# The attention rows of a chunk are transposed by DMA inside SBUF, and its query products stand in one run

## The chip, the cores and the metric

The kernel runs on one core of one Trainium2 chip. The metric is the device time of one execution in microseconds (us). Every time below is from that, or from one profiled execution of the same program.

## What is computed

The reference has three parts, one after another.

```python
# 1. linear attention: batch 8, heads 8, sequence 576, head width 64
kv = einsum('bhsd,bhse->bhde', k, v)
out = einsum('bhsd,bhde->bhse', q, kv)
out = out / sqrt(mean(out * out, axis=-1) + 1e-6) * g_norm
x = out.transpose(0, 2, 1, 3).reshape(4608, 512)
# 2. a dense layer with a maximum over three products, 512 -> 768 -> 512
h = maximum(maximum(x @ w1, x @ w2), x @ w3)
x = h @ w_out
# 3. a mixture of 8 experts, top 2 of noisy logits, 512 -> 1024 -> 512 each
out[token] = sum over its two experts of weight * (maximum(x @ W1[e], 0) @ W2[e])
```

## The kernel before

Tokens are worked on in nine chunks (0 to 8) of 512. Every matrix is split into a high part and a rest, and a product is taken as three products (high-high, high-rest, rest-high).

For a chunk, the dense layer has two stages. In the first, the loop over `g` makes 18 steps of 12 matmuls on TensorE (line 311, `g1_mm`). Three steps give one 128-wide slice of `h`: ScalarE copies the first step's bank into `hm`, VectorE takes the maximum with the next two, and `hsplit` splits the result (lines 315 and 319). Step 17 completes the last slice. In the second stage, `window(c)`, TensorE makes the output product for four blocks `i` of 128 tokens (line 357, `g2`, 36 matmuls each), and the results are copied out of their banks as 16-bit planes (line 364). Each `g2` block takes two of the four banks `AC`, in a ring (`abank`), so block 3 needs the banks of block 1.

The attention of chunk c+1 is worked in between during chunk c. `kv_pair` at step 10 makes the key-value matrix, `ao` multiplies it with the queries (line 214, 64 matmuls for half a chunk), `norm` scales the rows (`norm_a`: square on ScalarE and sum on VectorE; `norm_b1`, `norm_b2`: small operations; `norm_c`: scaling on VectorE), and `xtrans` brings the normed rows into the layout that the next first stage reads: four TensorE transposes into a bank (line 273), then a rounded copy on ScalarE (line 277) and a subtraction on VectorE (line 282). In chunks 1 to 7 half of the rows are made at step 14 and transposed in the window behind block 1; the other half's query products are in the window, and its rows are transposed in the middle of block 3. The order on each engine is the order of the program text; only chunk 0 has a planner. In chunk 1 the first stage works on 256 tokens, since the other 256 were done during chunk 0.

DMAs of the SP queue load queries (into the tile `RB`), keys and values (`KV0` and the tiles `G`) and the gate noise one chunk ahead. Pool's queue scatters the finished rows of a chunk into `Xg` in DRAM (line 427, at steps 10 and 14 of the next chunk) and, in chunk 2's program text, fills the output with zeros (`zero_out`, lines 540 and 543). In the third part `load_rows` reads rows back with a transposing DMA (line 755) as planes of 16-bit halves, and `utrans` copies these together again (line 790), rounds and subtracts (lines 793 and 794).

Of the kernel before, what the change touches and what calls it, by code (L numbers as in the profile page):

```python
# [7 lines left out]
F = mybir.dt.float32  # L8
# [4 lines left out]
U16 = mybir.dt.uint16  # L13
U64 = mybir.dt.uint64
AF = mybir.ActivationFunctionType
OP = mybir.AluOpType
# [4 lines left out]
NCH, CT = 9, 512  # L21
# [64 lines left out]
def body(tc, A, dbg=None):  # L86
    nc = tc.nc
    PE, ACT, DVE, POOL, SP = nc.tensor, nc.scalar, nc.vector, nc.gpsimd, nc.sync
# [8 lines left out]
    def st(name, shape, dt=F):  # L97
        return sb.tile(shape, dt, name=name)
# [5 lines left out]
    STG = [st(f"G{i}", [128, 2048]) for i in range(3)]  # L104
    B0, B1 = (st(f"B{i}", [128, 4096], FR) for i in range(2))
    B2 = st("B2", [128, 2048], FR)
    RA, RB = st("RA", [128, 4 * XW]), st("RB", [128, 4 * XW])
    KB = [sb1.tile([128, 256], F, name=f"kvt{i}") for i in range(2)]
    KV0 = sb1.tile([128, 2048], F, name="kv0")
# [4 lines left out]
    gn = st("gn", [128, 1])  # L114
# [9 lines left out]
    def hbank():  # L124
        cnt["h"] += 1
        return HB[(cnt["h"] - 1) % 4]

    def abank():
        cnt["a"] += 1
        return AC[(cnt["a"] - 1) % 4]  # L130
# [37 lines left out]
    def qv(c):  # L168
        return qbuf[c][:, 0:2048].rearrange("p (a t) -> p a t", a=4)
# [33 lines left out]
    def ao(c, j, banks):  # L203
        for h in range(2):
            ao_bank[c, 2 * j + h] = banks[h]
        for i in range(2):
            t0 = (2 * j + i) * 128
            for p in range(4):
                o = slice(i * 256 + p * 64, i * 256 + (p + 1) * 64)
                for x in range(2):  # L210
                    t = t0 + x * 64
                    kb = KB[(c * CT + t) // S % 2]
                    for h in range(2):
                        PE.matmul(banks[h][HALF[x], o], qv(c)[HALF[h], p, t:t + 64],  # L214
                                  kb[HALF[h], p * 64:(p + 1) * 64], start=True, stop=True)

    xn_of = {}
# [4 lines left out]
    def norm_a(c, i, x=None):  # L222
        if x is None:
            x = XNS[xn_n[0] % 4]
            xn_n[0] += 1
        norm_sq(c, i, x)
        norm_red(c, i)

    def norm_sq(c, i, x):
        xn_of[c, i] = x  # L230
        ACT.activation(x, ao_bank[c, i], AF.Square)
# [5 lines left out]
    def norm_b1(c, i0, i1):  # L237
        s = [ST[:, r, i0:i1, :] for r in range(2)]
        DVE.tensor_scalar(s[0], s[0], 1.0 / 64, 1e-6, op0=OP.mult, op1=OP.add)
        ACT.activation(s[1], s[0], AF.Ln)  # L240
        ACT.activation(s[1], s[1], AF.Exp, scale=-0.5)

    def norm_b2(c, i0, i1):
        s = [ST[:, r, i0:i1, :] for r in range(4)]
        DVE.tensor_tensor(s[2], s[1], s[1], op=OP.mult)
        DVE.scalar_tensor_tensor(s[2], s[2], -0.5, s[0], op0=OP.mult, op1=OP.mult)
        DVE.scalar_tensor_tensor(s[3], s[2], 1.5, s[1], op0=OP.add, op1=OP.mult)

    def norm_c(c, i):
        x = xn_of[c, i]  # L250
        DVE.tensor_tensor(x.rearrange("p (h e) -> p h e", h=8),
                          ao_bank[c, i].rearrange("p (h e) -> p h e", h=8),
                          ST[:, 3, i, :].unsqueeze(2).to_broadcast([128, 8, 64]), op=OP.mult)

    def norm(c, i, x=None):
        norm_a(c, i, x)
        norm_b1(c, i, i + 1)
        norm_b2(c, i, i + 1)
        norm_c(c, i)

    def xview(a, b):
        return [v.rearrange("p (k t) -> p k t", k=4) for v in (a, b)]

    xT = xview(B0[:, 0:2048], B0[:, 2048:4096])
# [20 lines left out]
    def xtrans(c, i):  # L285
        t = xtrans_pe(c, i)
        xtrans_hi(i, t)
        xtrans_lo(i, t)


    def split(src, w):
        ACT.activation(w[:, 0:1024], src, AF.Copy)  # L292
# [55 lines left out]
    def g2(c, i, f0, f1):  # L348
        if f0 == 0:
            x2b[i] = abank(), abank()  # L350
        s = slice(i * 128, (i + 1) * 128)
        for f in range(f0, f1):
            h = hTf(f)
            w = wo(f // 2)[:, :, f % 2]
            for n, (a, b) in enumerate(((0, 0), (0, 1), (1, 0))):
                for z, (lo, hi) in enumerate(((0, 256), (256, 528))):
                    PE.matmul(x2b[i][z][:, 0:hi - lo], h[:, a, s], w[:, b, lo:hi],  # L357
                              start=f == 0 and n == 0, stop=f == 5 and n == 2)
        if f1 == 6:
            DVE.tensor_copy(lgs[:, i, :], x2b[i][1][:, 256:272])  # L360
            for z in range(2):
                b = x2b[i][z].bitcast(U16).rearrange("p (n t) -> p n t", t=2)
                for q in range(2):
                    (ACT.copy if q else DVE.tensor_copy)(  # L364
                        planes[:, i, q * 512 + z * 256:q * 512 + z * 256 + 256], b[:, 0:256, q])
# [417 lines left out]
    def utrans(u, i, tight=False):  # L783
        s = slice(i * 128, (i + 1) * 128)
        pl = rplanes(u)
        g = MG[mgn[0] % 2]
        mgn[0] += 1
        h = g.bitcast(U16).rearrange("p (k t z) -> p k t z", k=4, z=2)
        for q in range(2):
            (ACT.copy if q and not tight else DVE.tensor_copy)(h[:, :, :, q], pl[:, 4 * q:4 * q + 4, s])  # L790
        t = g.rearrange("p (k t) -> p k t", k=4)
        x = xTu[u % 2]
        ACT.activation(x[0][:, :, s], t, AF.Copy)  # L793
        DVE.tensor_tensor(x[1][:, :, s], t, x[0][:, :, s].bitcast(F), op=OP.subtract)  # L794
        if i == units[u] - 1:
            m = units[u]
            DVE.tensor_copy(wid[u % 3][:, 0:m], gt[u % 3][:, 0:m, 0])
            DVE.tensor_copy(idt[u % 3][:, 0:m], gt[u % 3][:, 0:m, 1])
# [25 lines left out]
    def misc1(c, g):  # L824
        if c == 1 and g == 0:
            POOL.memset(STG[2][64:128, 0:1024], 0.0)
            fills()
        if c == 1 and (g == 0 or 8 < g < 14):
            f = max(g - 8, 0)
            hsplit(f, early(f), 0, 256)  # L830
        if c == 2 and g == 2:
            zero_out()
        if g == 0:
            SP.dma_start(noise[c % 2], A["noise"][c])
        if g == 0 and 0 < c < NCH - 1:
            load_q(c + 1)
            if c + 1 < NB:
                for i in range(3):
                    load_kv(c + 1, i)
        if c > 0:  # L840
            if g == 1:
                route_a(c - 1)
            if g == (7 if c == 1 else 10):
                route_b(c - 1)
                scatter(c - 1, 0)
            if g == (12 if c == 1 else 14):
                scatter(c - 1, 1)
        if 0 < c < NB - 1 and g == 10:
            bank = abank()
            for p in range(4):  # L850
                kv_pair(c + 1, p, bank)
            kv_out(c + 1, bank)
        if 0 < c < NCH - 1 and g == 14:
            ao(c + 1, 0, [abank(), abank()])
            for i in range(2):
                norm(c + 1, i)
        if c == NCH - 1:
            if g == 11:
                spec_pick()
                load_regs(0, spi[0:1, 0:1], spi[0:1, 1:2])  # L860
                regE[1] = regE[0]
                regS[1] = SP.value_load(spi[0:1, 2:3], min_val=0, max_val=DUMMY)
                for p in range(3):
                    load_pair(p)
            if g == 12:
                load_rows(0)
            if g in (13, 14, 15, 16, 17):
                splits(1)

    def window(c):  # L870
        nx = c + 1 < NCH

        def fill(i):
            if nx:
                if i == 0:
                    ao(c + 1, 1, [hbank(), hbank()])
                norm(c + 1, i + 2)

        def trans(i):
            xtrans(c + 1, i) if nx else utrans(0, i)  # L880

        if c == 0:
            for i in (2, 3):
                g2(0, i, 0, 3)
                trans(i)
                g2(0, i, 3, 6)
            xn_n[0] = 0
            return
        for i in range(4):
            g2(c, i, 0, 3)  # L890
            if nx and i == 3:
                trans(2)
                trans(3)
            g2(c, i, 3, 6)
            if nx and i == 1:
                trans(0)
                trans(1)
                fill(0)
                fill(1)
            if not nx:  # L900
                if i < 2:
                    trans(2 * i)
                    trans(2 * i + 1)
                if i == 1:
                    load_rows(1)
                splits(1)
# [15 lines left out]
    c = NCH - 1  # L922
# [337 lines left out]
```

## Time and profile before

| | us |
|---|---|
| median of 3 runs | 1556.95 (1556.66 to 1558.84) |
| the profiled execution | 1555.75 |
| its span in the trace | 1554.0 |
| TensorE busy | 1515.0 |
| VectorE busy | 792.4 |
| ScalarE busy | 646.0 |
| Pool busy | 221.4 |

The span is the time from the first to the last instruction in the trace. The busy time of an engine is the sum of its instructions; it is an average over stages. In the rows below, PE is TensorE, PEld its weight load, DVE VectorE, ACT ScalarE, POOL GpSimd and SP the queue that issues most DMAs.

### The profile page before, as it was taken

To read this page: it belongs to the slowest core of one execution; us is meant where nothing else is said; L and a number is where in the kernel's file an instruction comes from. 1 tells how busy PE (TensorE), PEld (TensorE's weight loads), DVE (VectorE), ACT (ScalarE), POOL (GpSimd) and SP (SyncE) were. 2 spreads that over 40 slices of the span, in tenths; PEclk is the share of its full clock that TensorE was granted. 3 is DMA by queue.
4 is the path that set the end of the run, shared out by engine and by line. 5 is a ranking of instruction groups with operands and counts; after the bars stand their busy time and mean duration, and the time that the engine had idled before them with its cause. 6 is when DMAs were issued, how large, how long until landed. Compare 5 with 4: busy or idle time off the path is not lost.

```text
span 1554.0 us, 23767 instructions
## 1 busy us (share of the span) xinstructions
PE 1515.0 (97%) x9564; PEld 1306.2 (84%) x9564; DVE 792.4 (51%) x1573; ACT 646.0 (42%) x1036; POOL 221.4 (14%) x326
## 2 busy tenths in 40 slices
PE   5999999999999999999999999999999999999997
PEld 4789989898989898888888787778888888888886
DVE  5985534343534343457454456465463554535443
ACT  3544322231313131343454445455464554645544
POOL 0000211111020202024211102101021010211102
PEclk8999999999999999999999999999999999999999
DMA  7322643031212101063676477766695666858554
GB/s 295 134 82 90 254 197 116 29 117 42 103 56 89 56 29 56 1 191 123 205 196 143 109 223 184 169 209 171 162 222 132 196 161 165 202 150 217 148 157 77
DMA packets 132292, 219.82 MB, mean 141 GB/s; under 512 B 96464, under 2 KB 96720, under 8 KB 114640
## 3 DMA queue, kind: packets, MB, share of 16 engines
q1 hardware_dynamic: 112320, 166.50, 34.0%
q0 software_dynamic: 19856, 51.73, 14.7%
q8 instruction: 77, 1.26, 0.3%
q14 instruction: 39, 0.32, 0.1%
HBM read 146.30 MB, written 51.72 MB: 127 GB/s over the span
## 4 chain that ended last, share of the span: by engine, by line
PE 92%; DVE 3%; ACT 2%; DMA 1%; issue 1%; POOL 1%; SPq 0%; POOLq 0%; ACTq 0%
PE bank L311 28%; PE bank L1068 24%; PE bank L1130 24%; PE bank L357 10%; PE bank L192 1%; PE bank L214 1%; PE bank L273 1%; DVE mg L790 1%; ACT B L793 1%; DMA pad<-kvr 1%; PE bank L1082 1%; DMA G<-kv 0%; POOL Xg L427 0%; DVE xlo L794 0%; PE bank L501 0%
## 5 line engine op out<-in xcount | busy, mean ns | idle before, releaser
L311 PE MATMUL bank<-B,W 128*128 128x512 f32 (+1 forms) x2160 | 455.5, 372 | 6.6 <-ACT W L482 4.2
L311 PEld LDWEIGHTS bank<-B,W 128*128 128x128 f32 x2160 | 377.6, 190 | 75.8 <-ACT W L482 4.9
L1130 PE MATMUL bank<-W,B 128*128 128x512 f32 x1728 | 423.3, 392 | 2.0 <-ACT xn L1135 1.9
L1130 PEld LDWEIGHTS bank<-W,B 128*128 128x128 f32 x1728 | 321.2, 189 | 67.0 <-ACT xn L1135 2.3
L1068 PE MATMUL bank<-B,W 128*128 128x512 f32 (+1 forms) x1728 | 355.0, 343 | 6.9 <-ACT B L793 6.9
L1068 PEld LDWEIGHTS bank<-B,W 128*128 128x128 f32 x1728 | 280.9, 190 | 51.1 <-ACT B L793 8.7
L293 DVE TENSOR_TENSOR W<-G,W 128x1024 fp32r<-128x1024 f32 x200 | 242.1, 1223 | 120.2 <-ACT W L292 119.6
L292 ACT ACTIVATE W<-G 128x1024 fp32r<-128x1024 f32 x200 | 207.6, 1055 | 53.3 <-PE bank L1130 39.8
L1073 DVE SCALAR_TENSOR_TENSOR B<-bank,B 128x512 fp32r<-128x512 f32 (+1 forms) x176 | 103.8, 592 | 207.1 <-ACT B L1072 206.6
L1072 ACT ACTIVATE B<-bank 128x512 fp32r<-128x512 f32 (+1 forms) x176 | 90.4, 516 | 266.7 <-PE bank L1068 265.5
L357 PE MATMUL bank<-W,B 128*128 128x256 f32 (+1 forms) x1296 | 164.0, 286 | 0.0
L357 PEld LDWEIGHTS bank<-W,B 128*128 128x128 f32 x1296 | 160.2, 188 | 1.1
L427 POOL DMA_INDIRECT Xg<-RA,si x72 | 72.1, 1001 | 522.1 <-issue 378.1
L329 DVE TENSOR_TENSOR hm<-hm,bank 128x512 f32<-128x512 f32 (+1 forms) x106 | 69.5, 656 | 132.3 <-PE bank L311 125.6
L315 ACT ACTIVATE B<-hm 128x512 fp32r<-128x512 f32 (+1 forms) x53 | 32.2, 607 | 184.7 <-DVE hm L329 184.7
L1068 PE MATMUL bank<-xlo,W 128*128 128x512 f32 x384 | 103.2, 391 | 0.0
L1104 POOL DMA_INDIRECT out<-xn,idt x37 | 61.3, 1655 | 275.3 <-ACT xn L1135 268.3
L1068 PEld LDWEIGHTS bank<-xlo,W 128*128 128x128 f32 x384 | 72.3, 188 | 15.1
L793 ACT ACTIVATE B<-mg 128x512 fp32r<-128x512 f32 x76 | 48.0, 632 | 84.4 <-DVE mg L790 84.3
L1104 POOL DMA_INDIRECT out<-x2T,idt x19 | 30.4, 1602 | 266.0 <-ACT x2T L1135 263.6
L364 ACT COPY RA<-bank 128x256 uint16<-128x256 uint16 x72 | 25.7, 372 | 88.0 <-DVE RA L364 72.7
L794 DVE TENSOR_TENSOR xlo<-mg,B 128x512 fp32r<-128x512 f32 x49 | 34.0, 694 | 36.7 <-ACT B L793 36.7
(184 smaller groups left out, 1010.4 us busy)
## 6 DMA issues: line engine op xcount, KB each, us to landing
G<-mw SPq DMA_DIRECT2D x100, 1024.0 KB, 5.1
G<-w1s SPq DMA_DIRECT2D x12, 1024.0 KB, 4.9
out<-pad POOLq DMA_DIRECT2D x1, 9472.0 KB
kv<-kv SPq DMA_DIRECT2D x8, 1024.0 KB, 7.2
G<-kv SPq DMA_DIRECT2D x8, 1024.0 KB, 9.7
RB<-qT SPq DMA_DIRECT2D x8, 1024.0 KB, 5.1
G<-kvr SPq DMA_DIRECT2D x7, 256.0 KB, 9.8
Xg<-RA,si POOLq DMA_INDIRECT x72, 2.7
```

Source lines behind the costliest of these rows:

```text
L292: ACT.activation(w[:, 0:1024], src, AF.Copy)
L293: DVE.tensor_tensor(w[:, 1024:2048], src, w[:, 0:1024].bitcast(F), op=OP.subtract)
L311: PE.matmul(bank[:, 0:t1 - t0], w_in(g)[:, a, k, s], x[b][:, k, t0:t1], start=n == 0 and k == 0, stop=n == 2 and k == 3)
L329: DVE.tensor_tensor(hm, hm, bank, op=OP.max)
L357: PE.matmul(x2b[i][z][:, 0:hi - lo], h[:, a, s], w[:, b, lo:hi], start=f == 0 and n == 0, stop=f == 5 and n == 2)
L427: i = POOL.indirect_dma_start(out=Xg, out_offset=bass.IndirectOffsetOnAxis(ap=idx, axis=0), in_=src, in_offset=None)
L793: ACT.activation(x[0][:, :, s], t, AF.Copy)
L1068: PE.matmul(bank[:, 0:n], w[:, a, k, s], x[b][:, k, 0:n], start=z == 0, stop=z == 11)
L1072: ACT.activation(h[:, 0, 0:n], bank[:, 0:n], AF.Relu)
L1073: DVE.scalar_tensor_tensor(h[:, 1, 0:n], bank[:, 0:n], 0.0, h[:, 0, 0:n].bitcast(F), op0=OP.max, op1=OP.subtract)
L1104: d = POOL.indirect_dma_start(out=A["out"], out_offset=bass.IndirectOffsetOnAxis(ap=idt[u % 3][:, i:i + 1], axis=0), in_=y, in_offset=None ...
L1130: PE.matmul(obank[i], h[:, a, s], w[:, b, ff % 2, :], start=ff == 0 and n == 0, stop=ff == 7 and n == 2)
```

## The change

From chunk 2 on, the TensorE transposes are gone. `planes_out` copies the low and the high 16-bit halves of a block of normed rows apart, into `KV0` (one half on VectorE, one on ScalarE). `planes_turn` issues a transposing DMA from `KV0` to `RB` on SP's queue, 128 partitions by 2048 halves, one for two blocks. `planes_in` puts the halves together again in a `G` tile and makes the rounded part and the rest from there. `attend` spreads the attention of a chunk over steps 12 to 15: all query products and the first two squares at 12, the other two and the small operations at 13, scaling and halves and a DMA at 14 and at 15. In the window `planes_in` comes behind output blocks 0 and 1. Chunks 0 and 1 keep the TensorE transposes.

```diff
+    def xplanes(c):
+        return [t.bitcast(U16)[:, 0:4096] for t in (KV0, RB)]
+
+    def planes_out(c, b):
+        d = xplanes(c)[0].rearrange("p (b z k i e) -> p b z i k e", b=4, z=2, k=2, i=2)
+        x = xn_of[c, b].bitcast(U16).rearrange("p (i k e z) -> p z i k e", i=2, k=2, z=2)
+        for z in range(2):
+            (ACT.copy if z else DVE.tensor_copy)(d[:, b, z], x[:, z])
+
+    def planes_turn(c, j):
+        src, dst = xplanes(c)
+        SP.dma_start_transpose(out=dst[:, j * 2048:(j + 1) * 2048].rearrange("p (q t) -> p q t", q=16),
+                               in_=src[:, j * 2048:(j + 1) * 2048])
+
+    def planes_in(c, b):
+        p = xplanes(c)[1].rearrange("p (b z n) -> p b z n", b=4, z=2)
+        m = STG[c % 2][:, b * 512:(b + 1) * 512]
+        h = m.bitcast(U16).rearrange("p (n z) -> p n z", z=2)
+        for z in range(2):
+            (ACT.copy if z else DVE.tensor_copy)(h[:, :, z], p[:, b, z])
+        j, k = divmod(b, 2)
+        m = m.rearrange("p (k t) -> p k t", k=2)
+        hi, lo = (x[:, 2 * k:2 * k + 2, j * 256:j * 256 + 256] for x in xT)
+        ACT.activation(hi, m, AF.Copy, scale=gn[:, 0:1])
+        DVE.scalar_tensor_tensor(lo, m, gn[:, 0:1], hi.bitcast(F), op0=OP.mult, op1=OP.subtract)
+
+    def attend(c, n):
+        if n == 0:
+            for j in range(2):
+                ao(c, j, [abank(), abank()])
+        if n < 2:
+            for b in (2 * n, 2 * n + 1):
+                norm_a(c, b)
+        if n == 1:
+            norm_b1(c, 0, 4)
+            norm_b2(c, 0, 4)
+        if n in (2, 3):
+            j = n - 2
+            for b in (2 * j, 2 * j + 1):
+                norm_c(c, b)
+                planes_out(c, b)
+            planes_turn(c, j)
...
-        if 0 < c < NCH - 1 and g == 14:
-            ao(c + 1, 0, [abank(), abank()])
-            for i in range(2):
-                norm(c + 1, i)
+        if 0 < c < NCH - 1 and g >= 12:
+            attend(c + 1, g - 12)
...
         for i in range(4):
-            g2(c, i, 0, 3)
-            if nx and i == 3:
-                trans(2)
-                trans(3)
-            g2(c, i, 3, 6)
-            if nx and i == 1:
-                trans(0)
-                trans(1)
-                fill(0)
-                fill(1)
+            g2(c, i, 0, 6)
+            if i < 2:
+                for b in (2 * i, 2 * i + 1):
+                    if nx:
+                        planes_in(c + 1, b)
+                    else:
+                        utrans(0, b)
```

## Rows read from the trace of the kernel before

**Rows 1.** The page, part 1: busy us, share of the span, instructions.

```profile
PE 1515.0 (97%) x9564; PEld 1306.2 (84%) x9564; DVE 792.4 (51%) x1573; ACT 646.0 (42%) x1036; POOL 221.4 (14%) x326
```

**Rows 2.** The chain that ended last, chunk 5: start us, us, what.

```profile
416.87 27.22 PE bank L311 x120
...
469.94 8.79 PE bank L357 x72
478.72 0.87 PE bank L273 x8
479.59 1.09 PE bank L214 x64
...
487.48 0.97 PE bank L273 x8
...
490.67 9.54 PE bank L311 x42
```

**Rows 3.** Groups by line: out<-in, shapes, count, busy us, mean ns, idle before.

```profile
L790 ACT COPY mg<-RB 128x512 uint16<-128x512 uint16 x41 | 31.6, 771 | 0.0
L790 DVE COPY mg<-RB 128x512 uint16<-128x512 uint16 x65 | 28.3, 455 | 0.0
...
L251 DVE TENSOR_TENSOR xn<-bank,stat 128x512 f32<-128x512 f32 x25 | 17.1, 691 | 2.3
...
L273 PE MATMUL bank<-cst,xn 128*128 128x128 f32 x100 | 15.3, 276 | 0.7 <-DVE xn L251 0.7
```

**Rows 4.** Busy time of each engine over chunk 5 (PE, PEld, DVE, ACT, POOL).

```profile
416.87:490.67 73.80, 73.80 (x587) 64.36 (x587) 31.39 (x94) 19.43 (x41) 8.42 (x16) 1.00 0.20 73
```

**Rows 5.** DMA queues from 699 to 704: GB/s by slice, packets and MB, landing us.

```profile
GB/s 0 0 0 0 0 0 0 0 0 0 0 0 0 0 16 111 156 102 162 201 256 233 268 291 291 285 293 291 291 289 291 293 285 291 293 291 289 289 295 285
...
q1 hardware_dynamic: 3142, 0.80, 72.5%
...
RB<-Xg SPq DMA_TRANSPOSE x1, 6.0
```

**Rows 6.** DMA issues from 671 to 683: us from issue to landing.

```profile
RB<-Xg SPq DMA_TRANSPOSE x1, 17.1
```

**Rows 7.** The chain that ended last, chunk 1's window and chunk 2's start.

```profile
174.81 8.79 PE bank L357 x72
...
195.53 4.55 PE bank L311 x20
```

**Rows 8.** Pool's timeline around 172: start us, us, instruction.

```profile
171.73 2.02 POOL L540 DMA_DIRECT2D out<-pad  x1
```

**Rows 9.** The page, part 6: sizes of Pool's two fills.

```profile
out<-pad POOLq DMA_DIRECT2D x1, 9472.0 KB
...
Xg<-pad POOLq DMA_DIRECT2D x1, 1040.0 KB
```

**Rows 10.** DMA queues from 174.6 to 182: packets, MB, share of 16 engines.

```profile
q0 software_dynamic: 735, 3.01, 101.6%
```

**Rows 11.** DMA issues from 185 to 191: KB, us to landing.

```profile
RB<-qT SPq DMA_DIRECT2D x1, 1024.0 KB, 11.1
```

**Rows 12.** The page, part 6: all such loads, median us to landing.

```profile
RB<-qT SPq DMA_DIRECT2D x8, 1024.0 KB, 5.1
```

**Rows 13.** DMA queues from 205 to 206: packets, MB, share of 16 engines.

```profile
q0 software_dynamic: 95, 0.39, 94.4%
q1 hardware_dynamic: 94, 0.02, 9.4%
```

**Rows 14.** DMA queues from 685 to 687.

```profile
q0 software_dynamic: 120, 0.41, 74.0%
q1 hardware_dynamic: 280, 0.07, 21.6%
```

**Rows 15.** TensorE's timeline around 31: start us, us, form, count, idle before.

```profile
30.95 5.55 PE L311 MATMUL bank<-B,W 128*128 128x512 f32 x16 [4.20 <-ACT W L482]
```

**Rows 16.** Busy time from 30 to 35; the seventh figure is the granted clock.

```profile
30.00:35.00 5.00, 4.05 (x11) 3.19 (x12) 4.92 (x7) 2.07 (x2) 0.00 (x0) 0.69 0.72 272
```

More of the change, by code (lines that the diff above doesn't have):

```diff
@@ L871, in window @@
         nx = c + 1 < NCH
[L873 to L880, printed above, removed]
         if c == 0:
@@ L884, in window @@
                 g2(0, i, 0, 3)
-                trans(i)
+                xtrans(1, i)
                 g2(0, i, 3, 6)
@@ L889, in window @@
         for i in range(4):
-            g2(c, i, 0, 3)
-            if nx and i == 3:
-                trans(2)
-                trans(3)
-            g2(c, i, 3, 6)
-            if nx and i == 1:
-                trans(0)
-                trans(1)
-                fill(0)
-                fill(1)
+            g2(c, i, 0, 6)
[5 more added lines that the diff above has]
+                        utrans(0, b)
             if not nx:
-                if i < 2:
-                    trans(2 * i)
-                    trans(2 * i + 1)
                 if i == 1:
```

## The prediction

> **What bounds the kernel.** I read the page first: TensorE (PE) is busy 97% of the span [rows 1]. A busy engine need not be the one that sets the end, so I then asked for the chain that ended last over one steady chunk, the fifth [rows 2]. Each piece begins where the one before ends, and every piece is PE: the big products, between them two passes over the queries (1.09 us each, one of them ahead of step 14) and two groups of transposes (0.87 and 0.97 us). One chunk is 490.67 - 416.87 = 73.80 us. So what leaves PE in such a chunk shortens the end by its own length, and what VectorE, ScalarE or a DMA gets to do costs nothing until PE has to wait for it.
>
> **Removed.** Chunks 2 to 8, seven of them, lose 16 transposes each. By the chain that is 0.87 + 0.97 = 1.84 us a chunk [rows 2], 12.9 us in all. The group's own mean of 0.276 us [rows 3] would give 4.4 us a chunk, but there transposes that follow each other overlap; I take the chain.
>
> **Moved.** The 128 query products of a chunk stand in one run before step 12. Twice 1.09 us stay 2.18 us: nothing.
>
> **Added on VectorE and ScalarE.** Each chunk has four 128x512 blocks. A block gets two 16-bit copies ahead of the DMA and two behind it, one of each pair on VectorE (0.455 us) and one on ScalarE (0.77 us) [rows 3]: 3.6 and 6.2 us a chunk. Over a whole chunk VectorE is busy 31.4 and ScalarE 19.4 of 73.8 us [rows 4]: there is room, and what counts is order. Let W be the moment at which PE starts the output product of the chunk before. A step of PE is 2.72 us (27.22 / 10, [rows 2]), so the run of query products ends at W-16.3. Squares and sums of the first two blocks follow it; those of the next two stand behind ScalarE's copy of step 12's bank, which waits for PE until W-13.6. Two squares and two sums (I take 0.6 to 0.7 us each, about a block's scaling of 0.69 [rows 3]), six small operations, then the maximum of step 13 bring VectorE to W-9.0. Two blocks of scaling and copying (0.69 + 0.455 each) and ScalarE's last copy: the first turn (the DMA transpose of blocks 0 and 1) goes out near W-6.3. Step 14's maximum and split and two more blocks: the second turn near W-2.0. By the end of step 17 VectorE is level with PE again, as before. No PE time.
>
> **The window's deadlines.** The copies behind a turn wait for it on VectorE and ScalarE, which go in order; queued behind them are the evictions of output block 1, whose two banks block 3 needs. Two blocks of copying back, rounding and subtracting (0.77, then about 0.65 and 0.69 each, partly side by side) take about 4.2 us, and an eviction about 1.3. Output block 3 starts three quarters into a product of 17.6 us, at W+13.2, so turn 0 has to land by about W+7.7. Turn 1 has to land by about W+13, for the next chunk's first product at W+17.6. These are 14 and 15 us after issue.
>
> **Price of a turn.** The trace has no transpose out of SBUF. The nearest row is one from DRAM: 512 rows x 1024 halves, 1 MB, landed 6.0 us after issue, in 256-byte packets, and flowed at 290 GB/s [rows 5]. A turn is half of that, 2048 packets: 1.8 us of flow, so 4 to 6 us. The upper end is 17.1 us, the longest landing of such a transpose, behind weight loads [rows 6]. I take 5, because the queues of a steady chunk are nearly idle at that place. Both turns then land by W+4 and are hidden. If that cover is gone, each us past the deadline is a us of PE in every chunk. On SP nothing comes late: behind the turns stand the next chunk's loads, which waited for PE's second query pass (9.7 us after W) and now wait for the copies back (about W+13), and are first read half a chunk later. Pool's queue is not passed.
>
> So six of the seven chunks give 6 x 1.84 = 11.0 us.
>
> **The seventh, chunk 2, meets something else.** Its turns go out during chunk 1, whose products are half as long (256 tokens, not 512). With all query products ahead of step 12, W moves from 174.81 [rows 7] by 1.09 to 175.9. The same walk, with steps of half the length, puts turn 0 at about 175.6 and turn 1 at 179.2. At 171.73 Pool starts the zero fill of the output [rows 8]: 9472 KB, and then 1040 KB more [rows 9]. From 174.5 on that fill holds the DMA engines: 735 packets of 4 KB in 7.4 us, 99 a us, 407 GB/s [rows 10]. Its 10.8 MB alone would last until 201; with the turns' 1 MB between them, until about 203.
>
> What does another queue get beside it? The query load issued at 185.65 landed after 11.1 us [rows 11], 6 us more than the 5.1 that is the median of such loads [rows 12]; I let turn 0 wait 5 us for its first packet. In the microsecond from 205 the fill moved 95 packets, and the other queue, then mostly the 128-byte rows of the noise, 94 [rows 13]: one for one, whatever the size. [...] A transpose beside another 4 KB stream is in the trace too: from 685 to 687 its queue got 280 packets beside 120 of a scatter, 140 a us [rows 14], though that scatter filled less of the engines' time (74%) than the fill does. So turn 0 flows for 2048/94 = 21.8 us as the dear bound, 2048/140 = 14.6 as a middle, 1.8 as the cheap bound (the fill does not hold it). I take the dear one: the fill keeps every engine full, as in [rows 13].
>
> Turn 0 then lands at 175.6 + 5 + 21.8 + 1 = about 204, when the fill ends, and turn 1 at 206. PE ends output block 2 near 191 and waits for block 1's banks: 204 + 4.2 + 1.3 + 4.4 (block 3 itself) = 213.9 for chunk 2's first product, which was at 195.53 [rows 7]: +18.3 us in place of -1.84. PE stands still for some 18 us. Early in the program, after an idle 4.2 us, 16 products took 5.55 us [rows 15]; at the pace of [rows 2] (120 in 27.22) they are 3.63. [...] That is 1.9 us lost; I add 2.0.
>
> **Sum.** -11.0 + 18.3 + 2.0 = +9.3 us on the profiled execution's 1555.75: 1565.0. The median shown is 1.2 above that execution, so 1566. A change under 0.2% (3.1 us) is about what a measurement of this kernel cannot tell from none.
>
> **Rivals.**
> *The turns slip past the fill* (the other side). If the engines serve a transpose's packets in bunches, turns 0 and 1 of chunk 2 land by about 188. Then chunk 1 costs only VectorE's crowding: step 17's split is ready near 181.0 and its output term is due at 179.6, 1.4 us. -12.9 + 1.4 = -11.5: 1545.5. For it: 140 a us in [rows 14] is more than one for one. Against it: [rows 13], and that the transpose of [rows 14] had slowed from 1131 a us (290 GB/s in packets of 256 bytes) to 140. It decides where turn 0 lands before about 195. Chance 0.22.
> *Held in part.* At 140 a us turn 0 lands at 196, turn 1 with the fill's end at 205, and the first product starts at 208.2, 3.2 us behind that: +12.7 + 2.0 - 11.0 = +3.7, so 1560.6; with more of the engines given to the turns, down to 1550. Chance 0.22.
> *Turns out of SBUF are slow in every chunk.* Both share one queue, so beyond 9.6 us each turn 1 misses W+13. At 17.1 each it lands at W+27.9: 15 us in each of six more chunks, near 1655. Against it: [rows 5], 32 blocks of 128x128 in 6.0 us. Chance 0.06. [...]
>
> **How the numbers follow.** My forecast has 0.50. Its own range is 1559 to 1571: from a little dearer than 140 a us up to a landing 3 us past the fill's end and a clock loss of 3.4. Over all cases the range goes down to the first rival: 1544 to 1571, with some 0.15 outside. Faster takes the first rival and the cheap end of the second, 0.26; same the middle of the second, 0.12; slower the rest, 0.62.
>
> **What would show it.** A period of 71.96 us from chunk 2 on; turns that land 4 to 6 us after issue in the later chunks; for chunk 2 a turn that lands after more than 20 us beside the fill, a copy on VectorE or ScalarE that waits for that DMA, a PE gap of 15 to 20 us ahead of output block 3 of chunk 1, and a lower granted clock behind it. The forecast is wrong if turn 0 of chunk 2 lands before 187, if the gap is absent, or if PE waits in any later window.

## The result, and the profile after

The changed kernel takes 1566.94 us (median of 5 runs, 1564.11 to 1568.15); the kernel before took 1556.92 beside it. The ratio is 1.0061, with a 95% interval of 1.0046 to 1.0076: slower by 10 us. The profiled execution took 1568.15 us, its span is 1566.3.

The page of the changed kernel, part 1 (busy us, share, instructions) and part 4 (chain that ended last, by engine), answers to [rows 1]:

```profile
PE 1506.7 (96%) x9452; PEld 1298.9 (83%) x9452; DVE 799.1 (51%) x1545; ACT 676.9 (43%) x1050; POOL 223.8 (14%) x326
...
PE 89%; DVE 3%; DMA 3%; ACT 2%; issue 1%; POOL 1%; SPq 0%; POOLq 0%; ACTq 0%; DVEq 0%
```

PE has 112 matmuls and 8 us less to do, and the span is 12 us longer: PE's share of the chain fell from 92 to 89% and a DMA's rose from 1 to 3%. So somewhere PE waits for a DMA. The chain from the end of chunk 1 to the first product of chunk 2 (start us, us, what) answers to [rows 7] and says where:

```profile
176.63 29.76 DMA RB<-kv
...
206.49 0.78 ACT G L310
...
211.25 0.38 ACT RA L407
...
211.68 7.16 PE bank L400 x36
218.84 1.38 PE bank L354 x6
```

It is read from below. Chunk 2's first product starts at 218.84, where it was 195.53. Ahead of it stands output block 3 of chunk 1 (7.16 us for 36 matmuls). Ahead of that is the eviction of block 1 (L407), behind ScalarE's copy of what the turn brought (L310), behind 29.76 us of the turn itself. The waits of the same kernel (who, for whom, us in total, times, longest) from 170 on name the same two hand-overs; PE waits nowhere else before the third part:

```profile
PE bank L400 <- ACT RA L407: 21.9, 1, 21.9
```
```profile
ACT G L310 <- DMA RB<-kv: 23.1, 1, 23.1
```

What holds the turn stands in the DMA queues of the changed kernel (packets, MB, share of 16 engines), from 185 to 200 beside the zero fill and from 206 to 207 after it. Pool's fill is on q0, both turns are on q1:

```profile
q0 software_dynamic: 1393, 5.71, 93.5%
q1 hardware_dynamic: 1394, 0.36, 10.5%
...
q1 hardware_dynamic: 1131, 0.29, 127.4%
```

In 15 us the fill moved 1393 packets and the turns' queue 1394: one for one. But the fill's hold 4096 bytes and the turns' 256, so the fill got 381 GB/s and the turns 24. As soon as the fill was out, the turns' queue moved 1131 packets in one microsecond, 290 GB/s, the pace of [rows 5].

A later chunk looks quite different. The chain from chunk 4's first product to chunk 5's answers to [rows 2], and below it stands the median landing of the ten turns issued from 290 to 650:

```profile
361.96 27.21 PE bank L354 x120
...
397.38 2.02 PE bank L214 x128
...
415.95 17.56 PE bank L400 x144
433.51 0.69 PE bank L354 x3
```
```profile
RB<-kv SPq DMA_TRANSPOSE x10, 4.9
```

The period is 433.51 - 361.96 = 71.55 us, against 73.80. The output product is one piece of 17.56 us with no transposes in it, the query products one of 2.02. PE waits for nothing.

### The profile page after: what moved, and what is told of

It is laid out like the page before. It is cut to its first block, busy times and chain, and to the rows that moved or that the text cites. A ratio compares the mean times of both kernels' runs of the same rounds, so it can differ in the third digit from the quotient of the medians.

```text
span 1566.3 us, 23588 instructions
## 1 busy us (share of the span) xinstructions
PE 1506.7 (96%) x9452; PEld 1298.9 (83%) x9452; DVE 799.1 (51%) x1545; ACT 676.9 (43%) x1050; POOL 223.8 (14%) x326
## 2 busy tenths in 40 slices
DMA packets 161412, 227.15 MB, mean 145 GB/s; under 512 B 125584, under 2 KB 125840, under 8 KB 143760
## 4 chain that ended last, share of the span: by engine, by line
PE 89%; DVE 3%; DMA 3%; ACT 2%; issue 1%; POOL 1%; SPq 0%; POOLq 0%; ACTq 0%; DVEq 0%
PE bank L354 27%; PE bank L1093 24%; PE bank L1155 24%; PE bank L400 9%; DMA RB<-kv 2%; PE bank L192 1%; PE bank L214 1%; DVE mg L833 1%; ACT B L836 1%; DMA pad<-kvr 1%; PE bank L1107 1%; DMA G<-kv 0%; POOL Xg L470 0%; DVE xlo L837 0%; PE bank L544 0%
## 5 line engine op out<-in xcount | busy, mean ns | idle before, releaser
L400 PE MATMUL bank<-W,B 128*128 128x256 f32 (+1 forms) x1296 | 163.0, 287 | 21.9 <-ACT RA L407 21.9
L407 ACT COPY RA<-bank 128x256 uint16<-128x256 uint16 x72 | 25.7, 372 | 68.6 <-DVE RA L407 62.8
L370 ACT ACTIVATE hm<-bank 128x512 f32<-128x512 f32 (+1 forms) x53 | 30.3, 572 | 56.7 <-PE bank L354 49.9
```

## The experiments

Each was run in turn with the kernel before on one chip, in two sets. There the kernel before took 1567.7 and 1567.6 us, 11 us more than in the first comparison (the result above; on which chip that ran is not on record). So only ratios and the parts of a trace are set beside each other. Expectations in us count from the first comparison's 1557.

**The fill held back.** Pool first reads one element that the last output block of chunk 1 writes, and then starts the fill.

```diff
-        if c == 2 and g == 2:
+        if c == 2 and g == 0:
+            POOL.tensor_copy(spacer, lgs[0:1, 3, 0:1])
             zero_out()
```

In the changed kernel:

> The changed kernel, with Pool's zero fill held back until chunk 1's last output block has been copied out (about the start of chunk 2). Theory (the fill, one packet for one, holds chunk 2's turns): both turns of chunk 2 land 4 to 6 us after issue, no PE gap ahead of output block 3 of chunk 1, and all seven chunks keep their gain of about 2.2 us, so 1541 to 1545 us. Rival (VectorE and ScalarE are crowded in chunk 1, whose steps are half as long): the place of the fill does not matter, the gap stays, about 1567. Rival (the first transposes out of SBUF are slow wherever they stand): the same, about 1567.

Measured: 1550.92 us, ratio 0.9885 (0.9870 to 0.9900). In ratios 0.990 to 0.992 had been expected; why it is more stands with the next experiment. Its chain, its turns' median landing, Pool's timeline and the fill's queue from 196 to 235:

```profile
168.41 2.02 PE bank L214 x128
...
179.27 17.57 PE bank L400 x144
196.84 27.21 PE bank L354 x120
...
268.39 6.81 PE bank L354 x30
```
```profile
RB<-kv SPq DMA_TRANSPOSE x2, 3.7
```
```profile
197.73 2.00 POOL L583 DMA_DIRECT2D out<-pad  x1 [0.37 <-issue]
```
```profile
q0 software_dynamic: 2656, 10.76, 67.8%
```

The same turns, at the same place in the text, now land after 3.7 us, and the output product of chunk 1 is one piece of 17.57 us. Both rivals of this experiment are out: chunk 1's crowding is still there, and these are still the first transposes out of SBUF. The fill's 10.76 MB now run beside chunk 2's first steps and delay nothing: that chunk takes 268.39 - 196.84 = 71.55 us, as a steady one. In the kernel before, the same edit:

> The kernel before, with only that one move of the fill. Theory: nothing in the old kernel waits for a DMA while the fill runs, so 1556 to 1558 us, no change. Rival (the place of the fill is worth time by itself, and the first experiment's gain is not the turns'): under 1552.

Measured: 1568.56 us, ratio 1.0002 (0.9989 to 1.0015). By itself the place of the fill is worth nothing that this interval (2 us either way) would show.

**One chunk, and all but one.** A condition chooses for each chunk between the old code and the new; the kernel without chunk 2 has `c > 2` in it.

```diff
+    def by_dma(c):
+        return c == 2
...
-        if 0 < c < NCH - 1 and g >= 12:
-            attend(c + 1, g - 12)
+        if 0 < c < NCH - 1 and by_dma(c + 1):
+            if g >= 12:
+                attend(c + 1, g - 12)
+        elif 0 < c < NCH - 1 and g == 14:
...
```

> Only chunk 2 goes by DMA, chunks 3 to 8 by TensorE as before; the fill where it was. Theory: the loss of chunk 2 stands alone, +21 to +25 us, so 1578 to 1582. Rival (the steady chunks lose the time): 1555 to 1559.

> Chunks 3 to 8 go by DMA, chunk 2 by TensorE as before; the fill where it was. Theory: six gains of 2.2 us alone, 1542 to 1545. Rival (whichever transposes out of SBUF come first are slow): chunk 3's turns take over 20 us and the time is about 1565.

Measured: chunk 2 alone 1584.72 us, 1.0103 (1.0088 to 1.0119), +17 us; all but chunk 2 1556.74 us, 0.9922 (0.9907 to 0.9937), -11 us. Both have the sign of the theory; -11 is a little less than the 12 to 15 expected, and its interval reaches from 10 to 15. Chunk 3, the first to be turned in the second kernel, is not slow. The chain with chunk 2 alone, and then that with all but chunk 2, each from the third step of chunk 1:

```profile
151.01 3.14 PE bank L354 x24
...
178.95 27.62 DMA RB<-kv
...
218.83 27.25 PE bank L354 x120
```
```profile
152.50 3.14 PE bank L354 x24
...
203.40 27.22 PE bank L354 x120
...
238.82 2.02 PE bank L214 x128
...
274.95 0.69 PE bank L354 x3
```

The third step of chunk 1 in the first comparison, in the kernel before and in the changed one:

```profile
151.73 3.14 PE bank L311 x24
```
```profile
152.62 3.13 PE bank L354 x24
```

Chunk 2 alone starts its first product at 218.83, as in the changed kernel of the first comparison (218.84). The loss is 17 us and not the 21 to 25 expected, because the old order itself is slower here in chunk 1. From the third step to chunk 2's first product the new order beside the fill took 66.2 us in the first comparison and takes 67.8 here. The old order took 43.8 us there (151.73 to 195.53) and takes 50.9 here (152.50 to 203.40). So in this stretch the loss was 22.4 us there and is 16.9 here. What slows the old order shows in the chain of the kernel before with the fill moved, around the query products of step 14, which take 1.09 us in [rows 2], and in the window behind the same pauses with all but chunk 2 (the seventh figure is the granted clock):

```profile
171.30 0.84 PE bank L214 x44
172.14 0.36 issue
172.50 0.36 PE bank L214 x6
...
204.21 27.22 PE bank L311 x120
...
277.98 1.15 PE bank L311 x5
```
```profile
175.40:182.69 7.29, 7.29 (x49) 7.29 (x49) 4.48 (x14) 2.34 (x7) 2.08 (x3) 0.77 0.81 326
```

PE pauses some 0.4 us after every four to six of these small products although it waits for nothing that the profile shows, and chunk 2 starts at 204.21 there. Behind such pauses the granted clock was 0.77 (1.00 at that place in the first comparison). The key-value products of step 10 have the same pauses in every trace of the two sets, with the old order and with the new. With the run at step 12 the query products take 2.02 us and have no such gaps (the chain of the fill held back, above). With the fill held back the stretch from the third step takes 43.7 us (153.18 to 196.84), 7.2 less than the old order here, where the old order of the first comparison took 43.8. So an estimated 5 us of what it gains on the kernel before (7.2 less the 2 us or so that a steady chunk gives) come from the pauses and not from the change's own saving. What the pauses are was not settled.

**A fill in half rows.** The intent was smaller packets of the fill beside the turn.

```diff
-        z = POOL.dma_start(A["out"]..., pad[:, 0:512]...)
+        for h in range(2):
+            z = POOL.dma_start(A["out"]...[:, :, h * 256:h * 256 + 256], pad[:, 0:256]...)
```

> The changed kernel with the zero fill cut into two DMAs of half rows (1 KB runs), at the old place. Theory (one packet of the fill for one of the turn): if the fill's packets shrink to 2 KB, turn 0 of chunk 2 flows at some 170 packets a us instead of 94 and lands about 10 us earlier, the PE gap shrinks from 22 to about 12 us, and the time falls by 8 to 11 us against the changed kernel. Rival (the queues share bytes or time, not packets): turn 0 lands as late as in the changed kernel, the same time within 3 us.

Measured: 1559.12 us, 0.9954 (0.9937 to 0.9972), and the changed kernel beside it:

> The changed kernel itself, beside the others on one chip. Theory: 1.004 to 1.008 of the kernel before. Rival (its loss belongs to the chip that it ran on first): 1.000 or less.

1571.17 us, 1.0032 (1.0017 to 1.0047), a little under the 1.004 to 1.008 expected: the kernel before has the pauses here. So the half rows took 12 us off the changed kernel, but not for the reason given. The queues from 185 to 188, Pool's timeline, the queue from 190.9 to 192 (no fill packet in it), PE's timeline, and PE's wait in the changed kernel beside it (from 150 to 690):

```profile
q0 software_dynamic: 277, 1.13, 95.1%
q1 hardware_dynamic: 276, 0.07, 10.3%
```
```profile
172.85 2.01 POOL L584 DMA_DIRECT2D out<-pad  x1
191.42 1.97 POOL L584 DMA_DIRECT2D out<-pad  x1 [16.56 <-issue]
```
```profile
q1 hardware_dynamic: 1250, 0.31, 126.8%
```
```profile
199.39 7.23 PE L400 MATMUL bank<-W,B 128*128 128x256 f32 x36 [7.96 <-ACT RA L407]
```
```profile
PE bank L400 <- ACT RA L407: 20.4, 1, 20.4
```

The fill's packets stayed at 4 KB (1.13 MB in 277), which is four runs of 1 KB, and the turns got one for one as before. But Pool started the second half only at 191.42, after the first was out, and in the pause between them the turns flowed freely (1250 packets in 1.1 us): PE's gap shrank from 20.4 to 7.96 us, by 12.4. This is the theory's cause with another lever. Why Pool waited is not shown. Whether smaller packets of the fill would give the turn more stays untried.

**The run alone.** All transposes stay on TensorE, the query products and norms go by the new order.

```diff
                 norm_c(c, b)
-                planes_out(c, b)
-            planes_turn(c, j)
...
+            g2(c, i, 0, 3)
+            if nx and i == 3:
+                xtrans(c + 1, 2)
+                xtrans(c + 1, 3)
+            g2(c, i, 3, 6)
+            if nx and i == 1:
+                xtrans(c + 1, 0)
+                xtrans(c + 1, 1)
...
```

> The new order alone: query products in one run at step 12, norms over steps 12 to 15, but all transposes on TensorE in the window as before. Theory (the transposes' PE time is the gain of a steady chunk, the run only 0.16 us of it): a period of about 73.6 us, 0.998 to 1.001 of the kernel before. Rival (the run is what gains): a period near 71.6 us, about 0.99.

Measured: 1564.11 us, 0.9978 (0.9967 to 0.9990). Its chain over chunk 2:

```profile
198.20 27.21 PE bank L352 x120
...
233.62 2.02 PE bank L214 x128
...
261.85 6.60 PE bank L398 x54
268.45 0.87 PE bank L273 x8
...
271.52 0.70 PE bank L352 x3
```

A period of 73.32 us. The kernel before has 73.77 on this chip (204.21 to 277.98 above, with the fill moved): the run gives 0.45 us, more than the 0.16 expected. The other 1.77 us to 71.55 go with the transposes. The ratio is no measure of this: without the pauses of step 14 chunk 2 starts 6.0 us earlier than at 204.21, and the third part, which is the same, takes 2.2 us longer (858.0 against 855.8).

**The version that beats both.** The changed kernel with the fill held back, once more beside the changed kernel:

> The changed kernel with the fill held back, once more, beside the changed kernel on the same chip. Theory: 0.988 to 0.992 of the kernel before, and some 1.5% under the changed kernel. Rival (the first gain was the other chip's): within 0.3% of the kernel before.

Measured: 1547.80 us, 0.9874 (0.9857 to 0.9892) of the kernel before, and 1547.80 / 1571.17 = 0.985 of the changed kernel. Of the 20 us against the kernel before some 5 belong to the pauses; the 23 us against the changed kernel, which runs its query products in the same place, do not. This version was not run beside the kernel before of the first comparison.

## Why the prediction was right, step by step

**Removed: right.** 1.84 us a chunk was forecast from the chain; 1.77 us is what the run-alone kernel and the changed kernel differ by. The group's mean (4.4 us) would have been far off.

**Moved: mis-sized.** The run was put at nothing and gives 0.45 us a chunk: 128 products together take 2.02 us instead of 2.18, and the pieces around the second pass become 0.3 us shorter (6.60 for 6.80, 0.87 for 0.97). The 6.80 is this line of the kernel before's chunk 5:

```profile
480.68 6.80 PE bank L357 x54
```

So six steady chunks gave 6 x 2.25 = 13.5 us, not 11.0.

**VectorE and ScalarE in the steady chunks: right.** The chain there is PE alone. In chunk 3 the first turn went out 6.75 us before the output product, forecast 6.3. The crowding of chunk 1 that the first rival priced at 1.4 us did not show: the output product with the fill held back is unbroken.

**A turn's own price: right.** 5 us was taken; 4.9 is the median in the changed kernel and 3.7 in quiet. The rival of slow turns in every chunk is out. The 14 turns brought 29,120 more packets (161,412 against 132,292), 2080 each, where 2048 were counted.

**Chunk 2: the cause right, each term a little short.** Turn 0 was issued at 176.63 (forecast 175.6), and up to 181.5 its queue moved nothing. From 181.5 to 182 it shows its first packets:

```profile
q1 hardware_dynamic: 4, 0.00, 0.9%
```

So the wait was 5 us, as taken, and then 93 packets went a us (1394 in 15), where 94 were taken from [rows 13]. Turn 0 landed after 29.8 us, forecast 27.8. PE's gap was 21.9 us, forecast 18; 1 us of that is a slip in the forecast, whose own W + 13.2 puts the end of block 2 at 189.1 and not near the 191 that it used (measured 189.8). Block 3 took 7.16 us, not 4.4 + 2.0. The changed kernel's windows over the gap, block 3 and what follows (the seventh figure is the granted clock) show why block 3 was slow:

```profile
190.00:211.68 21.68, 0.00 (x1) 0.00 (x1) 3.24 (x8) 3.29 (x6) 0.00 (x0) 0.58 0.88 279
211.68:218.84 7.16, 7.16 (x37) 7.11 (x38) 2.81 (x7) 3.81 (x7) 0.00 (x0) 0.62 0.44 160
218.84:230.00 11.16, 11.16 (x50) 9.22 (x50) 5.87 (x33) 4.56 (x9) 0.00 (x0) 1.00 0.53 203
```

After 21.9 us without a matmul block 3 ran at a granted clock of 0.62 of full. Before, 36 such matmuls took 4.40 us (half of the 8.79 for 72 in [rows 7]), and 4.40 / 0.62 is 7.1 us. In the stretch that the forecast took its 2.0 us from it was 0.69 [rows 16]. In all, chunk 2's first product came 23.3 us later than before; 0.9 of that was there at the start of chunk 1 (its third step began at 152.62, before at 151.73). So 22.4, against a forecast of 20.3.

**The sum: right, in part by luck.** Two errors offset each other: chunk 2's first product came 23.3 us late where 20.3 were forecast, and the steady chunks gave 2.5 us more than forecast. The first products of the third part, before and after, show what is left, 10.0 us:

```profile
702.29 8.17 PE bank L1068 x36
```
```profile
712.30 8.17 PE bank L1093 x36
```

The other 2.3 us of the two spans' difference arise in the third part, which the change does not touch. That part took 851.7 us before and 854.0 after; in the traces of the experiments it takes 854.8 to 858.2, though none of them touches it, so such a difference need have no cause in the change. The profiled execution was forecast at 1565.0 and took 1568.15; the median came out within 1 us of the 1566 forecast because the profiled execution lay 1.2 us above it this time and not below.

## What to carry to other kernels

A transposing DMA in small packets was cheap in a quiet moment (3.7 us) and in the steady chunks (4.9 us). Beside a bulk DMA with 4 KB packets it got one packet for one, a sixteenth of the bytes, and took 29.8 us. Before work moves from TensorE to a DMA, look through the DMA queues over the whole span for one-time bulk transfers, such as a zero fill, and not only at the steady loop. If one collides, try to move the bulk transfer (moving the transpose was not tried here); a small read of something that is written at the right time was enough to hold Pool back (its fill was issued at 197.73, in the changed kernel at 172.72).

## What the runs showed of the hardware

Beside the fill the two queues shared the DMA engines by packets and not by bytes: 1393 to 1394 over 15 us in the changed kernel, 277 to 276 over 3 us with the fill in half rows. What that came to in bytes (381 GB/s beside 24 in the changed kernel) followed from the size of a packet on each side, which the trace gives: 256 bytes for the transpose, 4096 for Pool's fill, even where its runs were cut to 1 KB (1.13 MB in 277 packets).

A transpose out of SBUF went no slower than the one from DRAM in [rows 5]: 290 GB/s in the changed kernel's microsecond from 206, and 512 KB landed 3.7 us after issue with the fill held back.

A second DMA of 4736 KB on Pool's queue started after an idle 16.56 us of Pool, at 191.42, when the first had drained (no fill packet from 190.9 to 192). That was not expected, and the pause it left accounts for the gain of the half-row fill (PE's gap 12.4 us shorter, the time 12).
